# The second feed-forward walked by weight groups, with accumulators kept on chip and an order made from one stored key for each task

## Chip, cores and metric

One core of a Trainium2 chip. The metric is the device time of one execution in microseconds (us), and lower is better. The kernel before takes 879.63 us, the median of three runs (878.31 to 879.94).

## What is computed

Attention with a threshold below each row's maximum, then two feed-forward networks, one after the other, on the same 2304 tokens:

```python
scores = q @ k.T / sqrt(64)                    # 4 batches, 8 heads, 576 tokens, 64 wide
scores = where(scores >= max(scores) - tau, scores, -1e9)
x = softmax(scores) @ v                        # then heads side by side: [2304, 512]

h = x @ w_in                                   # first network, 512 -> 1024
solu = h * softmax(h)
x = layer_norm(solu) * g_ln @ w_out            # 1024 -> 512

h = x @ w2_in                                  # second network, 512 -> 2048
out = (h * tanh(softplus(h))) @ w2_out         # 2048 -> 512
```

All inputs are float32. The weights w_in, w_out, w2_in, w2_out come as 64-bit floats and are converted on chip.

## The kernel before

**Words.** A product that must keep float32 accuracy is made of three matmuls on rounded parts (high times high, low times high, high times low). A value is split by a copy on ScalarE (ACT) that rounds, and a subtraction on VectorE (DVE) or GpSimd (POOL) that leaves the low part.

**Three stages that overlap.** Attention (`s_tile`, `turn`, `pv`) writes its result to DRAM, `xd`. The first network (`moe_h`, `layer_norm`, `moe_t`, `moe_y`) reads it in tiles of 128 tokens and writes `yc`. The second network (`ff_in`, `ff_out`) is the subject of the change. Attention's early matmuls on `st` (pairs of half-height operands, 64 rows), its `pv` matmuls (half-width results, tile `V`) and all the rest are the three modes of TensorE (PE) that the planner knows.

**The second network.** Each of its two matrix products is a block product of 2x2 blocks with seven block products in place of eight. So the weights and the inputs are stored as seven combinations each: `yc` for the inputs (three units u of 768 tokens, seven tiles `y` of 768 KB for each), `w2c` for the weights. The 2048 inner columns are cut into eight groups g. `ff_in(z, g)` makes the activated combinations `gh` and `gl` of one group from seven `y` tiles and seven weight tiles `A` (256 KB each, stored as high and low words): 7 products of 6 matmuls, 128x384. `ff_out(v, q)` multiplies two groups (q is a pair of groups, 0 to 3) with 14 weight tiles `B`: 14 products of 6 matmuls. A `B` tile is stored raw (128 KB), so each load is followed by a copy on ACT (L1039) and a subtraction on DVE (L1041). The sums are added to four accumulators `acc` for a unit by DVE (L1136); the first one is a copy by ACT (L1134).

**The walk.** `VISITS` lists which unit is on chip and which pairs q it goes through:

```python
VISITS = (0, (0,1)), (1, (1,0)), (2, (0,1,2,3)), (0, (3,2)), (1, (2,3))
```

Units 0 and 1 come twice. At the end of their first visit the accumulators go to DRAM (`part`), at the start of the second they are loaded again. A set of `A` or `B` tiles is kept only from one step to the next (`AL.clear()`, `BL.clear()`). The seven `y` tiles have a ring of seven and two more, `y7x`, from the second visit on; `A` has 8 buffers, `B` 20, `acc` 5.

**The order.** No engine's order is written by hand. Each piece is a task with an engine, a duration and its needs, and `Plan.run` makes a list schedule: the engine that can start first takes the ready task with the best key, and the instructions are issued in that order. The keys come from forty turns of a forward and a backward pass, and the table `REFINE` then shifts some of them. A slot of a ring is taken to be free when the user as many places before it is done. All DMAs of the three stages are issued from one queue, SyncE's (SP), in the planned order, so a DMA that waits for its data or its buffer holds all behind it.

Of the kernel before, what the change touches and what calls it, by code (L numbers as in the profile page):

```python
# [80 lines left out]
class Plan:  # L81
# [28 lines left out]
    @staticmethod  # L110
    def lag(d, t):
        if d.eng == t.eng:
            return 0.0 if t.eng in ("PE", "-") else 0.13
        return 0.0 if d.eng == "SP" else 0.2 if d.eng == "PE" else 0.27 if t.eng == "PE" else 0.16

    def ranks(self):

        for t in self.tasks:
            t.left, t.key = len(t.out), 0.0
        ready = [t for t in self.tasks if not t.left]  # L120
        while ready:
            t = ready.pop()
            t.key += t.dur
            for d, data in t.need:
                far = (0.2 if d.eng != t.eng else 0.0) + (2.0 if d.eng == "SP" else 0.0) if data else 0.0
                d.key = max(d.key, t.key + far)
                d.left -= 1
                if not d.left:
                    ready.append(d)
# [27 lines left out]
    def moved(self, order):  # L157

        digits = "ABCDEFGHIJKLMNOPQRSTUVWXYZabcdefghijklmnopqrstuvwxyz0123456789+/"
        for z in range(0, len(REFINE), 4):  # L160
            x = 0
            for c in REFINE[z:z + 4]:
                x = 64 * x + digits.index(c)

            def draw():
                nonlocal x
                x = (x * 1103515245 + 12345) & 0x7FFFFFFF
                return x >> 8

            draw()  # L170
            middle, half, rare = draw() % len(order), 20 + draw() % 400, 1 + draw() % 5
            size = (1.0, 3.0, 10.0, 30.0)[draw() % 4]
            for t in order[max(0, middle - half):middle + half]:
                if draw() % (1 << rare) == 0:
                    t.key -= size * (draw() % 2001 - 1000) / 500.0
# [73 lines left out]
    def backward(self):  # L249

        free, port, dma, mode = {}, 0.0, 0.0, 0
        for t in self.tasks:
            t.after, t.before = [], []
# [974 lines left out]
```

## Time and profile before

| | |
|---|---|
| runs | 878.31, 879.63, 879.94 us |
| the profiled execution | span 879.3 us, from its first to its last instruction, within the range of the runs |
| TensorE (PE) matmuls | 848.3 us busy, 96% of the span |
| VectorE (DVE) | 766.1 us busy, 87% |
| ScalarE (ACT) | 609.4 us busy, 69% |
| GpSimd (POOL) | 328.9 us busy, 37% |
| DMA | 195.21 MB, 222 GB/s over the span |
| chain that ended last | PE 69%, DVE 15%, DMA 6%, ACT 4% |

The first row of the second network on PE stands at 426.7 us, the last matmul of the first network ends at 520.7 us. A PE that is busy for 96% of a span is not at its peak for that time: a matmul's row lasts longer than the distance to the next one. What counts on PE is how many matmuls there are, at what distance they follow each other, and where the row is empty.

### The profile page before, as it was taken

The numbers are of one execution on the slowest core, as the hardware profiler recorded it, in microseconds if no ns is written. First come the engines' busy times: TensorE is split into PE (matmuls) and PEld (weight loads), VectorE is DVE, ScalarE is ACT, GpSimd is POOL, SyncE is SP. The second block draws the span as 40 slices with busy tenths as digits, with TensorE's granted clock in tenths as the row PEclk, the third lists the DMA queues.
The fourth block names the chain that finished last, engine by engine and source line by source line (L and its number), as shares of the span: only waits on it lengthen the run. The fifth ranks groups of instructions, "written<-read, shape, count | busy, mean of one in ns | idle before, by whom it ended". The sixth has DMA issues, their size and how long they took to land.

```text
span 879.3 us, 16385 instructions
## 1 busy us (share of the span) xinstructions
PE 848.3 (96%) x5423; PEld 736.9 (84%) x5423; DVE 766.1 (87%) x1638; ACT 609.4 (69%) x1292; POOL 328.9 (37%) x370
## 2 busy tenths in 40 slices
PE   8899999999999999999999998999989999999998
PEld 4556666778787887978897898999989999999997
DVE  7998998879888899997778899999999997788877
ACT  5889998779878978866556867765656565455442
POOL 3677767556765574544134211112311201010100
PEclk9999999999999999999999999999999999999999
DMA  7667543354735546376996689999998768787541
GB/s 226 196 198 211 158 145 127 96 157 127 216 102 168 183 144 222 91 221 191 372 361 188 198 286 318 356 367 385 352 326 261 236 204 271 236 312 248 199 156 72
DMA packets 155573, 195.21 MB, mean 222 GB/s; under 512 B 15313, under 2 KB 112609, under 8 KB 155489
## 3 DMA queue, kind: packets, MB, share of 16 engines
q1 hardware_dynamic: 155344, 194.17, 67.9%
q8 instruction: 43, 0.70, 0.3%
q14 instruction: 42, 0.34, 0.1%
q10 hardware_dynamic: 144, 0.00, 0.0%
HBM read 142.94 MB, written 51.19 MB: 221 GB/s over the span
## 4 chain that ended last, share of the span: by engine, by line
PE 69%; DVE 15%; DMA 6%; ACT 4%; issue 3%; POOL 2%; SPq 0%; ACTq 0%; POOLq 0%; DVEq 0%
PE hoa L1012 22%; PE p_mo L846 10%; PE p_mo L916 8%; PE hob L1012 7%; PE p_ta L789 6%; PE p_ta L739 5%; PE st L702 4%; PE st L694 4%; DVE e L712 2%; DVE gl L1100 2%; DVE ws L605 2%; DVE acc L1136 1%; DVE m L708 1%; DMA B<-w2c 1%; PE p_mo L895 1%
## 5 line engine op out<-in xcount | busy, mean ns | idle before, releaser
L1012 PE MATMUL hoa<-y,A 128*128 128x384 f32 x696 | 136.3, 338 | 2.1 <-DMA A<-w2c 1.0
L1072 POOL TENSOR_TENSOR gf<-gf 128x384 f32<-128x384 f32 x24 | 33.9, 1411 | 252.7 <-DVE gf L1072 252.7
L1012 PEld LDWEIGHTS hoa<-y,A 128*128 128x128 f32 x696 | 121.9, 189 | 4.1 <-ACT gf L1062 1.8
L712 DVE SCALAR_TENSOR_TENSOR e<-st,m,e 128x576 f32<-128x576 f32 x139 | 111.2, 812 | 12.9 <-ACT e L709 7.3
L708 DVE TENSOR_REDUCE m<-st 128x1 f32<-128x576 f32 x139 | 102.3, 751 | 19.8 <-PE st L702 10.7
L709 ACT ACTIVATE e<-st,m 128x576 f32<-128x576 f32 x139 | 101.6, 744 | 20.6 <-DVE m L708 19.7
L1012 PE MATMUL hoa<-gh,B 128*128 128x384 f32 x436 | 111.5, 336 | 1.6 <-DVE acc L1136 1.4
L1100 DVE TENSOR_TENSOR gl<-gf,gh 128x384 fp32r<-128x384 f32 x168 | 93.8, 598 | 0.7 <-ACT gh L1098 0.4
L739 PE MATMUL p_ta<-ident,e 128*128 128x128 f32 x576 | 83.7, 277 | 3.5 <-DVE e L712 1.2
L916 PE MATMUL p_mo<-LH,W2H 128*128 128x256 f32 x288 | 83.9, 291 | 0.0
L739 PEld LDWEIGHTS p_ta<-ident,e 128*128 128x128 f32 x576 | 65.1, 140 | 20.9 <-ACT ey L720 3.7
L916 PE MATMUL p_mo<-LL,W2H 128*128 128x256 f32 x288 | 81.4, 283 | 0.0
L916 PE MATMUL p_mo<-LH,W2L 128*128 128x256 f32 x288 | 81.3, 282 | 0.0
L1012 PEld LDWEIGHTS hoa<-gh,B 128*128 128x128 f32 x436 | 78.4, 188 | 3.5 <-DVE acc L1136 2.8
L1098 ACT ACTIVATE gh<-gf 128x384 fp32r<-128x384 f32 x168 | 78.2, 514 | 4.4 <-DVE gf L1072 2.5
L1068 ACT ACTIVATE gf<-gf 128x384 f32<-128x384 f32 x72 | 37.5, 523 | 57.7 <-DVE gf L1065 57.6
L1012 PE MATMUL hoa<-gl,B 128*128 128x384 f32 x218 | 73.6, 337 | 3.6 <-DVE gl L1100 3.6
L711 POOL TENSOR_SCALAR m<-m,cs 128x1 f32<-128x1 f32 x144 | 51.4, 359 | 64.9 <-DVE m L708 51.0
L555 POOL TENSOR_TENSOR ws<-cf,cl 128x512 uint32<-128x512 uint32 x32 | 46.3, 1446 | 73.3 <-DMA w2c<-ws 37.5
L846 PE MATMUL p_mo<-W1H,XH 128*128 128x512 f32 x144 | 61.3, 426 | 1.8 <-DVE LL L901 1.8
L1012 PE MATMUL hob<-gh,B 128*128 128x384 f32 x236 | 60.6, 338 | 0.4 <-DVE acc L1136 0.4
L1136 DVE TENSOR_TENSOR acc<-acc,hoa 128x384 f32<-128x384 f32 x93 | 50.2, 548 | 11.4 <-PE hoa L1012 9.7
(127 smaller groups left out, 2244.1 us busy)
## 6 DMA issues: line engine op xcount, KB each, us to landing
A<-w2c SPq DMA_DIRECT2D x140, 256.0 KB
y<-yc SPq DMA_DIRECT2D x28, 768.0 KB
w2c<-ws SPq DMA_DIRECT2D x32, 448.0 KB
B<-w2c SPq DMA_DIRECT2D x112, 128.0 KB
cr<-w_in SPq DMA_DIRECT2D x32, 256.0 KB
cr<-w_out SPq DMA_DIRECT2D x32, 256.0 KB
yc<-yh SPq DMA_DIRECT2D x9, 896.0 KB
yc<-ys SPq DMA_DIRECT2D x9, 896.0 KB
```

What stands on the lines that cost most here:

```text
L708: t = add("DVE", dve(S), lambda: V.tensor_reduce(m.tile[:, 2:3], x(), AX.XY, ALU.max, negate=True), [t], [m], [st])
L709: a = add("ACT", act(S, True) + 0.1, lambda: SC.activation(et(), x(), ACTF.Exp, bias=m.tile[:, 2:3]), [t], [e] if h == 0 else (), [st, m, ...
L711: b = add("POOL", 0.26, lambda: G.tensor_scalar(m.tile[:, 1:2], m.tile[:, 2:3], -1.0, nt8, ALU.mult, ALU.add), [t], use=[m])
L712: t = add("DVE", dve(S) + 0.06, lambda: V.scalar_tensor_tensor(et(), x(), m.tile[:, 1:2], et(), ALU.is_ge, ALU.mult, accum_out=sr.tile[:, ...
L739: TE.transpose(tp.tile[:, k * 128:(k + 1) * 128], e.tile[:, o:o + 128], ident)
L789: TE.matmul(acc.tile[h * 64:h * 64 + 64, :w], v.tile[:, k, h], r, start=(k == 0), stop=(k == KT))
L846: TE.matmul(h.tile, l.tile[:, kt], r[:, kt, j * 512:(j + 1) * 512], start=(kt == 0 and x == 0), stop=(kt == KD - 1 and x == 2))
L916: TE.matmul(y.tile[:, :PN], l[:, k, cs], r.tile[:, k], start=(k == 0 and x == 0), stop=(k == KF - 1 and x == 2))
L1012: TE.matmul(x.tile[:, :TH], l, r, start=new and n == 0, stop=stop and n == len(steps) - 1, skip_group_check=True)
L1098: a = add("ACT", act(TH), lambda h=h, x=x: SC.activation(h.tile, full(x), ACTF.Copy), [first], [h], [h, x])
L1100: out[c] = h, l, add(e, cost(TH), lambda h=h, l=l, x=x, eng=eng: eng.tensor_tensor(l.tile, full(x), f(h.tile), ALU.subtract), [a, *deps], ...
L1136: d = add("DVE", dve(TH), lambda: V.tensor_tensor(to(), to(), fr(), ALU.add), deps + [CO.get((v, e, i, t))], use=[ac, x])
```

## The change

Nothing of the arithmetic changes: PE has the same matmuls in the same numbers (2016 of them in the second network). Four things change.

1. The walk. Each pair q is now visited by all units before the next pair begins, and the direction turns at the ends, so each step changes either the unit or the pair. There are nine visits instead of five. Every set of `A` and `B` tiles is loaded once (group 0 of `A` twice), the `y` tiles at each visit.
2. The buffers. Twelve accumulators stay on chip: eight in `acc`, four in the buffers `ys` and `yh` of the first network. `part` is gone. `A` has 8 buffers and 7 more (`A7x`, in the pool that opens when the first network is done), `B` 16, and `y` a single ring of seven.
3. The planner. One pass with stored keys, one for each task (`KEYS`), takes the place of forty turns and `REFINE`. A slot is free when any earlier user is done. Transfers have rates by row size, a first delay of 0.95 and a last of 1.5 us, and at most eight are under way; a change of PE's mode counts 0.24 us (before 0.1).
4. Some durations of tasks.

```diff
-    TURNS = 40
-    WAITS = 20.0, 250.0
-    ISSUE, LATENCY = 0.65, 0.92
-    LOAD, AVOID = 1.3, (3.0, 30.0, 150.0)
-    DRAIN = 0.1
+    RULE = 250.0, 3.0
+    ISSUE, FIRST, LATENCY = 0.48, 0.95, 1.5
+    LANES = 8
+    LOAD = 1.3
+    DRAIN = 0.24
...
+        for z, t in zip(range(0, len(KEYS), 3), self.tasks):
+            a, b, c = (place[k] for k in KEYS[z:z + 3])
+            t.key = (a * 4096 + b * 64 + c - 65536) / 64.0
...
+                for x in t.takes:
+                    at = max(at, min(x.buf.free, default=1.0e9))
...
-                free["SP"] = b + self.ISSUE
-                dma = max(free["SP"] + self.ISSUE, dma) + t.dur
+                dma = max(b + self.FIRST, dma) + t.dur
                 t.end = dma + self.LATENCY
+                lanes.append(t.end)
+                lanes.pop(0)
+                free["SP"] = max(b + self.ISSUE, lanes[0])
...
-    NA, NB, NL, NR, NX, NC, NF = 8, 20, 13, 14, 2, 5, 8
+    NA, NB, NL, NR, NC, NF = (8, 7), 16, 13, 14, 8, 7
...
-    b_a, b_b = (buf(p, n, [128, 2, 256], F32R, k) for p, n, k in (("fa", "A7", NA), ("fc", "B7", NB)))
-    b_y, b_yx = (buf(p, n, [128, 2, TU // PN, 2, 128], F32R, k) for p, n, k in (("fa", "y7", 7), ("fc", "y7x", NX)))
-    ring_y = [b_y] * 7
+    b_a, b_ax, b_b = (buf(p, n, [128, 2, 256], F32R, k) for p, n, k in (("fa", "A7", NA[0]), ("fc", "A7x", NA[1]), ("fc", "B7", NB)))
+    b_y = buf("fa", "y7", [128, 2, TU // PN, 2, 128], F32R, 7)
...
-    VISITS = (0, (0,1)), (1, (1,0)), (2, (0,1,2,3)), (0, (3,2)), (1, (2,3))
+    VISITS = (0, (0,)), (1, (0,)), (2, (0, 1)), (1, (1,)), (0, (1, 2)), (1, (2,)), (2, (2, 3)), (1, (3,)), (0, (3,))
...
+    for u in (0, 1):
+        for i in range(2):
+            for e in range(2):
+                ac = b_ac.new()
+                AC[u, e, i] = ac, lambda ac=ac: ac.tile
+    for e in range(2):
+        last = (b_ys, b_yh)[e].new()
+        for i in range(2):
+            AC[2, e, i] = last, lambda last=last, i=i: f(last.tile.rearrange("p c n -> p (c n)"))[:, i * TU:(i + 1) * TU]
...
-        A = AL.pop(g, None) or [load_w(b_a, 0, g, c, o_a) for c in range(7)]
-        AL.clear()
-        AL[g] = A
+        if g not in AL:
+            early = z == 0 or g % 2
+            AL[g] = [load_w(b_a if early else b_ax, 0, g, c, o_a if early else o_c) for c in range(7)]
+        A = AL[g]
...
-        Bs = BL.pop(q, None) or {(c, g): load_w(b_b, 1, g, c, o_c) for c in range(7) for g in gs}
-        BL.clear()
-        BL[q] = Bs
-        if begins:
-            for e in range(2):
-                for i in range(2):
-                    ac = AC[v, e, i] = b_ac.new()
-                    if more[0]:
-                        CO[v, e, i, 0] = CO[v, e, i, 1] = add("SP", dma(512 * TU), lambda ac=ac, e=e, i=i: D(ac.tile, part[u][e + 2 * i]),
-                                                              [PA[u, e, i], o_c], [ac])
+        if q not in BL:
+            BL[q] = {(c, g): load_w(b_b, 1, g, c, o_c) for c in range(7) for g in gs}
+        Bs = BL[q]
```

In numbers of instructions, counted in the order of both programs: `y` loads 35 and 63, `A` loads 140 and 63, `B` loads 112 and 56 and with each one copy on ACT and one subtraction on DVE, stores to `part` 8 and 0, loads from it 8 and 0. The additions to accumulators (144 on DVE, 24 copies on ACT), all else on DVE, ACT and POOL, and every matmul stand in both as often. TensorE changes its mode 125 times before and 110 times now.

**First place: PE early in attention.** L694 and L722 are the early half-height matmuls, L789 and L817 `pv`, L742 to L739 and L767, L770 transposes through `ident`. Before:

```order
L789 MATMUL p_ta_328<-ex,V 64x256 x8
L789 MATMUL p_ta_328<-eu,V 64x256 x2
L742 MATMUL p_ta_356<-ident,e 128x128
L694 MATMUL s_360<-Kst,Qhh 128x256
L694 MATMUL s_360<-Kst,Qhh 128x320
L739 MATMUL p_ta_368<-ident,e 128x128 x4
L739 MATMUL p_ta_379<-ident,e 128x128 x4
L694 MATMUL st<-Kst,Qhh 128x320
L694 MATMUL st<-Kst,Qhh 128x256 x2
L694 MATMUL st<-Kst,Qhh 128x320
L742 MATMUL p_ta_406<-ident,e 128x128
```

And of the change, at the same place of the program:

```order
L817 MATMUL p_ta_324<-ex,V 64x256 x8
L817 MATMUL p_ta_324<-eu,V 64x256 x2
L767 MATMUL p_ta_356<-ident,e 128x128 x4
L767 MATMUL p_ta_364<-ident,e 128x128 x4
L722 MATMUL s_375<-Kst,Qhh 128x256
L722 MATMUL s_375<-Kst,Qhh 128x320
L722 MATMUL st<-Kst,Qhh 128x320
L722 MATMUL st<-Kst,Qhh 128x256 x2
L722 MATMUL st<-Kst,Qhh 128x320
L770 MATMUL p_ta_394<-ident,e 128x128
```

The transposes no longer stand between two groups of half-height matmuls: five changes of mode have become three.

**Second place: PE where the first network ends and the first `ff_out` begins.** L916 and L944 are the last matmuls of the first network, L1012 and L1039 the second network's. Before:

```order
L916 MATMUL p_mo_6786<-LL,W2H 128x256
L1012 MATMUL hoa_6020<-y_5783,A_6624 128x384 x6
L1012 MATMUL hoa_6895<-y_5678,A_6681 128x384 x6
L1012 MATMUL hoa_6020<-y_5802,A_6672 128x384 x6
L1012 MATMUL hoa_6736<-y_5794,A_6644 128x384 x6
L1012 MATMUL hoa_6941<-y_5688,A_6699 128x384 x6
L1012 MATMUL hoa_6955<-y_5738,A_6792 128x384 x6
L1012 MATMUL hoa_6988<-gh,B_6893 128x384 x2
L1012 MATMUL hoa_6988<-gl,B_6893 128x384
```

And of the change:

```order
L944 MATMUL p_mo_6797<-LL,W2H 128x256
L1039 MATMUL hoa_6242<-y_5963,A_6581 128x384 x6
L1039 MATMUL hoa_6001<-y_5974,A_6623 128x384 x6
L1039 MATMUL hoa_6878<-y_6731,A_6028 128x384 x6
L1039 MATMUL hoa_6750<-y_6253,A_6013 128x384 x6
L1039 MATMUL hoa_6928<-y_6086,A7x 128x384 x6
L1039 MATMUL hob_6945<-y_6240,A7x 128x384 x6
L1039 MATMUL hoa_6750<-y_6757,A_6560 128x384 x6
L1039 MATMUL hob_6977<-gh,B_6861 128x384 x2
L1039 MATMUL hob_6977<-gl,B_6861 128x384
```

Seven products of `ff_in` instead of six now stand ahead of the first one with `B`, and the fifth and sixth of them read `A7x`, whose pool, like that of `B`, opens only when the first network is done.

**Third place: PE in the middle of the second network, where one `y` tile follows another in the same buffer.** `y_9467` of unit 2 takes the buffer that `y_9062` of unit 1 leaves. Of the change:

```order
L1039 MATMUL hoa_9233<-y_9062,A_8685 128x384 x6
L1039 MATMUL hoa_9458<-gh,B_8990 128x384 x2
L1039 MATMUL hoa_9458<-gl,B_8990 128x384
L1039 MATMUL hoa_9458<-gh,B_8995 128x384 x2
L1039 MATMUL hoa_9458<-gl,B_8995 128x384
L1039 MATMUL hoa_9233<-y_9110,A_8725 128x384 x6
L1039 MATMUL hoa_9480<-y_9271,A_9383 128x384 x6
L1039 MATMUL hoa_9233<-y_9137,A_8762 128x384 x6
L1039 MATMUL hoa_9257<-y_9123,A_8750 128x384 x6
L1039 MATMUL hoa_9515<-y_9467,A7x 128x384 x6
```

Between the last matmul on the old tile and the first on the new one stand 30 matmuls. Eight of the 56 reloads of `y` have 30 to 36 matmuls between, the others more. Before, the ring of nine left two tiles to run ahead.

## Rows read from the trace of the kernel before

**Rows 1.** Stretches of core 0: busy us by engine, granted clock, DMA share, GB/s

```profile
0.00:175.00 175.00, 164.93 (x1088) 107.76 (x1090) 155.53 (x337) 147.23 (x301) 111.85 (x160) 1.00 0.55 170
175.00:417.00 242.00, 236.89 (x1728) 199.12 (x1726) 212.35 (x453) 192.82 (x390) 138.61 (x156) 1.00 0.54 165
417.00:528.00 111.00, 108.28 (x703) 98.00 (x701) 90.99 (x202) 71.39 (x136) 30.18 (x22) 1.00 0.84 280
528.00:550.00 22.00, 19.46 (x101) 18.96 (x101) 19.85 (x44) 16.70 (x42) 2.50 (x2) 0.92 0.93 319
550.00:700.00 150.00, 144.91 (x818) 141.02 (x817) 145.20 (x314) 94.48 (x220) 30.42 (x21) 1.00 0.96 326
700.00:880.00 180.00, 173.84 (x996) 172.03 (x994) 142.17 (x293) 86.74 (x207) 15.32 (x12) 1.00 0.64 213
```

**Rows 2.** Waits of PE from 525 to 880 us: total, times, longest

```profile
PE hoa L1012 <- DVE gl L1100: 3.6, 3, 2.5
PE hoa L1012 <- ACT gf L1062: 1.4, 2, 0.9
PE hoa L1012 <- DVE acc L1136: 1.4, 2, 0.9
PE hoa L1012 <- DMA A<-w2c: 1.0, 1, 1.0
PE hob L1012 <- ACT gf L1062: 0.9, 1, 0.9
```

**Rows 3.** The chain that ended last, in order of time, 520 to 535 us

```profile
522.29 4.78 DMA B<-w2c
...
527.10 0.77 ACT B L1039 x2
...
530.47 0.48 DVE gl L1100
```

**Rows 4.** Groups of instructions on DVE, 550 to 700 us: busy, mean ns

```profile
L1100 DVE TENSOR_TENSOR gl<-gf,gh 128x384 fp32r<-128x384 f32 x70 | 41.1, 630 | 0.1
L1041 DVE TENSOR_TENSOR B<-B 128x256 fp32r<-128x256 f32 x44 | 19.6, 464 | 0.0
...
L605 DVE TENSOR_TENSOR ws<-ws 128x128 f32<-128x128 f32 x45 | 12.6, 282 | 0.1
```

**Rows 5.** DMA issues over the whole span, with KB each

```profile
A<-w2c SPq DMA_DIRECT2D x140, 256.0 KB
y<-yc SPq DMA_DIRECT2D x28, 768.0 KB
...
B<-w2c SPq DMA_DIRECT2D x112, 128.0 KB
...
part<-acc SPq DMA_DIRECT2D x8, 384.0 KB
```

**Rows 6.** A lone load: SP's timeline 791 to 794 us

```profile
792.26 0.32 SPq L1028 DMA_DIRECT2D y<-yc  x1
```

**Rows 7.** DMA by 40 slices of 0.125 us, 792 to 797 us

```profile
DMA  2210000005699910919697999929241040999095
```

**Rows 8.** The chain, 740 to 757 us

```profile
743.23 6.17 DMA y<-yc
...
750.48 5.92 DMA A<-w2c
```

**Rows 9.** Timeline of weight loads at a change of mode, near 11 us

```profile
10.92 0.30 PEld L694 LDWEIGHTS st<-Kst,Qhh 64*128 64x128 f32 x4 [0.17 <-issue]
```

**Rows 10.** Waits of weight loads, 0 to 525 us

```profile
PEld st L694 <- issue: 10.7, 30, 2.5
```

**Rows 11.** The chain, 690 to 712 us

```profile
697.79 7.28 PE hoa L1012 x42
```

More of the change, by code (lines that the diff above doesn't have):

```diff
@@ L111, in lag @@
     def lag(d, t):
[L112 to L129, printed above, removed]
+        if d == t:
+            return 0.0 if t in ("PE", "-") else 0.13
+        return 0.0 if d == "SP" else 0.2 if d == "PE" else 0.27 if t == "PE" else 0.16
     def place(self, choose, put, first):
@@ L214, in put @@
                 bank[x.bank] = None
+            for x in t.takes:
+                x.buf.free.remove(min(x.buf.free))
             if t.port:
@@ L234, in put @@
                     stale.add("PE")
+            for x in t.drops:
+                x.held -= 1
+                x.latest = max(x.latest, t.end + max(self.lag(t.eng, e) for e in x.buf.eng))
+                if not x.held:
+                    x.buf.free.append(x.latest)
+                    stale.update(x.buf.eng)
             for k in t.opens:
@@ L247, in forward, with run @@
         return done if self.place(choose, put, first) else None
[L249 to L251 removed]
+    def run(self):
+        self.shared, self.banks, self.groups, self.rings, self.slots = [], [], [], [], []
         for t in self.tasks:
[L253 to L301 removed]
@@ L303, in run @@
-    def run(self):
-        self.shared, self.banks, self.groups = [], [], []
-        for t in self.tasks:
-            t.bank, t.back, t.uses, t.out, t.leads, t.opens = None, None, [], [], [], []
+            t.bank, t.back, t.uses, t.out, t.opens, t.takes, t.drops = None, None, [], [], [], [], []
         for t in self.tasks:
@@ L318, in run @@
                     continue
-                if x.k >= b.bufs:
-                    t.need += [(u, True) for u in b.slots[x.k - b.bufs].users]
+                t.takes.append(x)
+                self.slots.append(x)
+                for u in x.users:
+                    u.drops.append(x)
                 if x.k:
                     t.need.append((b.slots[x.k - 1].taker, False))
+                if b not in self.rings:
+                    self.rings.append(b)
+                    b.eng = set()
+                b.eng.add(t.eng)
         for k in self.banks:
@@ L588, in words7 @@
             out.append((a, b))
-        return [add("SP", dma(128 * 7 * n * 4), lambda w=w, y=y: D(dst(w), f(y.tile)), [o[w] for o in out], use=[y]) for w, y in ((0, hi), (1, x))]
+        return [add("SP", dma(128 * 7 * n * 4, n * 4), lambda w=w, y=y: D(dst(w), f(y.tile)), [o[w] for o in out], use=[y]) for w, y in ((0, hi), (1, x))]
     WLO = V, "DVE", dve
@@ L1158, in ff_out @@
                     r0 = (e + 2 * i) * 128
-                    to = (lambda e=e, i=i: part[u][e + 2 * i]) if more[1] else (lambda r0=r0: out[r0:r0 + 128, u * TU:(u + 1) * TU])
-                    PA[u, e, i] = add("SP", dma(512 * TU), lambda e=e, i=i, to=to: D(to(), AC[v, e, i].tile),
-                                      [CO[v, e, i, t] for t in range(2)], use=[AC[v, e, i]])
+                    add("SP", dma(512 * TU, 4 * TU), lambda e=e, i=i, r0=r0: D(out[r0:r0 + 128, u * TU:(u + 1) * TU], AC[u, e, i][1]()),
+                        [CO[u, e, i, t] for t in range(2)], use=[AC[u, e, i][0]])
     MINUS = [{'D': ('DVE', dve(TH)), 'P': ('POOL', gps(TH))}[k] for k in 'DPDD']
@@ L1168 @@
         for q in qs:
-            for g in (2 * q + 1, 2 * q) if q == qs[0] and z else (2 * q, 2 * q + 1):
+            for g in (1, 0) if z == 1 else (2 * q, 2 * q + 1):
                 ff_in(z, g)
             ff_out(z, q)
+            if z == 0:
+                AL.pop(0)
     plan.run()
```

303 lines of the change are left out of this document (165 added, 138 removed).

## Prediction

> **What bounds the kernel now.** I read the stretches first. PE is busy almost throughout: in six stretches [rows 1] it is empty for 10.1, 5.1, 2.7, 2.5, 5.1 and 6.2 us (each stretch less its busy time), 31.7 us in 880, of which the last few are the final stores. The matmuls of the second network follow each other at 7.28 / 42 = 0.173 us [rows 11], and the change takes none away. So PE's work is the floor, and only its waits, its mode changes and a low clock can be won: some 30 us at most, plus whatever hides inside rows that count as busy.
>
> Who is waited for differs by stretch. From 550 to 700 us DVE is busy for 145.2 of 150 us and the DMA engines for 0.96 of the time, at 326 GB/s [rows 1]: both are full where PE loses its 5.1 us. The list of PE's waits in the second network [rows 2] names DVE (gl, acc) and ACT (gf), and only once a DMA, 1.0 us for an A tile. The chain shows the start of that stage: the first B tiles, 4.78 us of DMA, their copy on ACT, then gl [rows 3]. PE's longest wait there, 2.5 us [rows 2], comes right before the only stretch with a low clock: 0.92 granted over 22 us [rows 1]. With levels of 2.4 and 1.2 GHz that is 22 x 0.08 / 0.5 = 3.5 us at the lower one, so about 1.8 us lost.
>
> **The change part by part**, against the profiled execution's own 879.3 us (the median of the runs is 879.63, so nothing is to be added).
>
> *Traffic.* A loads fall by 77 of 256 KB, B loads by 56 of 128 KB, 16 transfers of 384 KB to and from part go, and 28 loads of y at 768 KB are added [rows 5]: -20.2 - 7.3 - 6.3 + 22.0 = -11.8 MB of 195. That is 36 us of a full DMA at 326 GB/s, but only a single 1.0 us wait of PE is put down to an A load [rows 2]: I count **-1.0** for it, and the room goes to the y loads below.
>
> *DVE and ACT.* 56 subtractions of B go, and as many copies on ACT. In the full stretch 44 of the 112 stand, 0.464 us each [rows 4]; half of them are 10 us of 145. It is not all gain: the conversions of the second network's weights (L605 and others, [rows 4]) now run on until the last pair is needed, so some move into the stretch where B left. What PE waited for DVE and gf outside the first 2.5 us is 1.1 + 1.4 + 1.4 + 0.9 = 4.8 us [rows 2]. Bounds 0 and -4.8; DVE should fall from 97% to about 91%, which thins the waits without ending them: I take **-3.0**. On ACT, 69% busy overall, the copies cost nothing now, being covered by ACT's slack.
>
> *First ff_out.* Before, 36 matmuls (6.2 us) separate the end of the first network from the first product with B; now 42 (7.3 us), and the B chain has 1.0 us more. But the two A7x products stand 24 and 30 matmuls behind that end, 4.2 and 5.2 us. Their loads open at the same event as B's and take the next places on SP. A B load took 4.78 us there [rows 3], so the first A7x is likely to be 1 to 2 us late. Before, 2.5 us of wait and 1.8 us of clock were lost; I keep 2.0: **-2.3** (bounds -4.3 and +1, the latter if the wait is as long again and the clock falls as before).
>
> *The y ring of seven.* This is where the change adds a wait. Eight reloads have 30 to 36 matmuls, 5.2 to 6.2 us, between the last use of the old tile and the first of the new. What a load takes is in two rows: alone on the queue, issued at 792.26 [rows 6], its bytes move until slice 33 of 40, 796.1 us [rows 7]: 3.9 us. Behind others it was 6.17 us until the waiting step was released [rows 8]. So a reload costs 0 or about 1.0 us, 0 to 8 in all; behind it the whole product queue on PE waits, then gf and gl. Reloads with more matmuls between are covered by the ff_out between them, 84 matmuls or 14.6 us, against 7 x 0.79 MB / 326 GB/s = 16.9 us of transfer for a whole unit, spread over a longer time since tiles come free one by one. Most loads there meet others on the queue, but less than before: I take **+3.0**.
>
> [...]
>
> *Mode changes.* 15 fewer. A weight load right after a change stood idle for 0.17 us [rows 9]; over the 30 waits of this kind the mean is 10.7 / 30 = 0.36 us [rows 10]. So 2.6 to 5.4 us; I take the lower, since the larger mean also holds other waits: **-2.6**.
>
> *The new order of the first 528 us.* Attention and the first network do the same work in another order. PE is empty there for 10.1 + 5.1 + 2.7 = 17.9 us [rows 1]. DVE is at 89% in the first 175 us, so the softmax chain is the limit and no order removes it all. The planner's transfers are nearer to the lone load above (a first delay of 0.95 us; in [rows 7] the bytes start in slice 9, at 793.1, 0.87 us after the issue), which should help, but the order was found on a model all the same. Bounds: half the idle time won, -9, or 5 lost. I take a quarter, **-4.5**.
>
> *At no cost:* the copy and addition counts are equal, and the accumulators in ys and yh only need the first network to be done with them, which it is before the first ff_out of unit 2.
>
> Sum: -1.0 - 3.0 - 2.3 + 3.0 - 2.6 - 4.5 = -10.4, so 879.3 - 10.4 = **868.9 us**.
>
> **The rivals.**
>
> *The y reloads are the new bound (slower).* The nine buffers were two tiles of slack, now there is none, and each of the nine visits reloads all seven tiles. For it: a load behind another 768 KB takes 2.4 us more at 326 GB/s, and an A tile of a third the size took 5.92 us behind y loads [rows 8]. Against it: rows 2 name no y load as a wait now, and 11.8 MB are gone. If each of the eight reloads is late by 1.0 us and half a load more, 2.2 us, and two visits in addition lose 2 us at wider gaps, the term is 21.6 instead of 3: 887.5 us. It decides from a term of 13.4 us on, 1.7 us for each of the eight.
>
> The Trainium skill speaks on the same side: "Double-buffer for performance" ("Trainium Kernel Development and Optimization", Best Practices). As a mechanism of this kernel that is the case just worked out; no row of before can show it, since the ring of nine ran ahead.
>
> *DVE stays the limit.* The conversions fill the room that B leaves, and the early order gives only 2 us: -1.0 - 2.3 + 3.0 - 2.6 - 2.0 = -4.9, so 874.4 us. For it: DVE at 97% [rows 1] with many kinds of work; against it: 56 x 0.464 = 26 us less in all.
>
> *Everything works.* All of DVE's waits go, no y load is late, and half of the early idle time is won: -1.0 - 4.8 - 4.3 - 2.6 - 9.0 = -21.7, so 857.6 us. For it: the y loads start as early as the lone one, and the DMA is emptier. Against it: it needs three terms at their ends.
>
> *Nothing to measure.* The early order loses what the second network wins: a term of +5 there instead of -4.5 gives 878.4 us.
>
> **How the numbers follow.** The forecast's own case, 863 to 873 us, gets 0.44. Everything works, under 863: 0.18. DVE the limit, 873 to 877.9: 0.13. Within 0.2% (1.8 us, about what a measurement of this kernel can tell from no change): 0.08. Slower, by the y reloads or by an early order that is worse: 0.17. So faster 0.75, same 0.08, slower 0.17. The range leaves out a tenth at each end: under 857, where three terms stand at their best ends, and over 883, where the y term is near 17 us. It is 857 to 883; that of the likeliest case is 863 to 873.
>
> **What would show it.** In the profile of the changed kernel: about 26 us less DVE busy and less on ACT by 56 copies, and DVE in the middle of the second network near 91%, with fewer waits for gl and acc. Waits of PE for y loads, new, a few of about 1 us, 3 us in total; much more of them is the first rival. A wait of 1 to 2 us for A7x at the end of the first network, and no stretch there with a lower clock. 110 mode changes, and an idle time of PE in the first 528 us near 13 us. The forecast is wrong if the early idle time has grown, since no row of before tells how good the new order is, or if waits for y reach 1.7 us each.

## The result and the profile after

The changed kernel takes 886.38 us (median of six runs, 884.39 to 887.89) where the kernel before takes 878.97: a ratio of 1.0087, 95% interval 1.0065 to 1.0109. It is slower by some 7.4 us; the forecast was 868.9, and 886 lies outside its range. One of the six runs before, 1035.49 us, is a slow one that the ratio leaves out; without it the median before is 878.31. The profiled execution spans 884.4 us, before 879.3.

The stretches up to 700 us, as in [rows 1]:

```profile
0.00:175.00 175.00, 162.84 (x1083) 109.89 (x1083) 151.70 (x329) 142.72 (x289) 113.61 (x156) 1.00 0.55 171
175.00:417.00 242.00, 237.90 (x1715) 199.36 (x1716) 214.88 (x456) 198.43 (x400) 137.71 (x157) 1.00 0.53 161
417.00:528.00 111.00, 103.92 (x684) 92.89 (x683) 79.96 (x175) 63.41 (x126) 29.42 (x20) 0.98 0.80 270
528.00:550.00 22.00, 18.44 (x102) 18.12 (x101) 17.83 (x32) 15.71 (x37) 3.65 (x3) 0.92 0.96 327
550.00:700.00 150.00, 147.69 (x836) 144.02 (x835) 139.07 (x294) 89.61 (x195) 26.35 (x20) 1.00 0.82 277
```

PE is empty for 12.2, 4.1, 7.1, 3.6 and 2.3 us there; before it was 10.1, 5.1, 2.7, 2.5 and 5.1. In the first 528 us that makes 23.4 us in place of 17.9. The second network at 550 to 700 us got better, as forecast, with an emptier DMA and a DVE at 139 of 150 us. The stretch from 417 to 528 us got worse by 4.4 us, and the clock is low in two stretches (0.98 and 0.92) in place of one: in the trace it stands at the lower of its two levels for 3.4 us from 520.6 us on, behind a wait of 1.9 us, and again for 3.4 us from 537.7 us on, behind a wait of 3.6 us.

PE's waits from 525 us on, as in [rows 2]:

```profile
PE hoa L1039 <- ACT gf L1096: 4.1, 2, 3.6
PE hoa L1039 <- DMA y<-yc: 1.0, 2, 0.9
...
PE hob L1039 <- DMA y<-yc: 0.4, 1, 0.4
```

So PE's wait for `gl`, which hung on `B` before [rows 2, 3], is gone, waits for y loads come to 1.4 us, and a new one of 3.6 us stands first. What it is made of is in the chain around it (start, duration, what):

```profile
529.72 1.06 PE hoa L1039 x6
...
533.02 1.27 DVE gf L1106
534.29 1.55 DVE gl L1134
...
535.86 0.50 ACT gf L1096
...
536.40 1.90 PE hoa L1039 x8
```

PE has no more to do until ACT has copied a first product of the next `ff_in` group (L1096, `copy`), and that copy waits for `gl` of the group before. What `gl` sets free is a `gf` buffer. ACT's own waits from 410 to 560 us name the same pair; before there is no such row in that stretch:

```profile
ACT gf L1096 <- DVE gl L1134: 4.0, 3, 2.2
```

And before that, PE's waits from 417 us on have five of 0.7 us or more in the first network (lines 874 and 923). They are for the layer norm's result (`so`, L904), for the low part of the network's input (`XL`, L863) and for two copies of PE's results out of their banks (L957, L881):

```profile
PE p_mo L923 <- POOL so L904: 2.5, 2, 1.3
PE p_mo L923 <- ACT ys L957: 1.0, 1, 1.0
PE p_mo L874 <- POOL XL L863: 0.7, 1, 0.7
PE p_mo L923 <- ACT so L881: 0.7, 1, 0.7
```

**Where the time went.** Both profiles hold 5423 matmuls. If each record counts with the usual distance of its form to the next one (0.173 us for `ff_in` and `ff_out`, 0.228 for L874 and 0.120 for L944, and so on), the records give how far PE has come, and the time lost is the time passed less the work done; PE's waits are in it, and what a low clock costs. From one profile each, with the runs told of below:

```
time lost (us) when PE has done ... us of its work
                                 400    475    500    550    650    800
before                          41.3   45.0   50.2   50.8   58.7   60.7
changed                         40.2   50.8   56.4   57.0   62.3   66.7
e1_gf8                          39.9   51.0   54.3   54.9   59.3   63.9
e3_head                         42.1   48.1   50.6   51.7   57.1   62.6
e4_head_gf8                     40.2   45.9   50.0   51.0   54.3   59.9
e8_fillers                      40.0   45.1   47.6   49.2   53.7   58.9
s2_new_walk_searched            44.3   47.2   52.6   53.8   56.1   57.3
x1_join_406                     41.5   44.7   49.9   51.3   54.3   55.5
```

400 us of work are the attention and some of the first network (440 us of time), 475 about its end, 475 to 500 the junction, where the first `ff_out` begins. Up to 400 the changed kernel is 1.1 us ahead; from 400 to 475 it loses 10.6 us where before lost 3.7; in the junction 5.6 against 5.2; from 550 on 9.7 against 9.9. Each low spell of 3.4 us is an estimated 1.7 us of this (half of it): one in the 10.6, one in the 5.6, and one in the 5.2 of before. A start can differ by 2 us between executions (e3 and e4 walk the same order up to 400), so differences between columns tell more than a column.

### The profile page after: what moved, and what is told of

Read it like the earlier page. It is cut to its first block, busy times and chain, and to the rows that moved or that the text cites. A ratio compares the mean times of both kernels' runs of the same rounds, so it can differ in the third digit from the quotient of the medians.

```text
span 884.4 us, 16090 instructions
## 1 busy us (share of the span) xinstructions
PE 849.1 (96%) x5423; PEld 739.0 (84%) x5423; DVE 753.4 (85%) x1582; ACT 596.3 (67%) x1234; POOL 330.7 (37%) x370
## 2 busy tenths in 40 slices
DMA packets 138146, 183.39 MB, mean 207 GB/s; under 512 B 13376, under 2 KB 103504, under 8 KB 138064
## 4 chain that ended last, share of the span: by engine, by line
PE 65%; DVE 16%; ACT 8%; DMA 5%; issue 3%; POOL 2%; SPq 1%; DVEq 0%; POOLq 0%; ACTq 0%
PE hoa L1039 22%; PE p_mo L944 9%; PE hob L1039 8%; PE p_mo L874 8%; PE p_ta L817 5%; PE p_ta L767 4%; PE st L730 4%; PE st L722 3%; DVE e L740 2%; DVE gl L1134 2%; ACT e L737 2%; DMA y<-yc 1%; DVE m L736 1%; PE p_mo L923 1%; DMA Qhh<-qq 1%
## 5 line engine op out<-in xcount | busy, mean ns | idle before, releaser
L1039 PE MATMUL hoa<-gh,B 128*128 128x384 f32 x488 | 124.5, 335 | 1.0 <-DVE acc L1161 0.6
L1106 POOL TENSOR_TENSOR gf<-gf 128x384 f32<-128x384 f32 x24 | 29.4, 1226 | 229.7 <-DVE gf L1106 229.7
L1132 ACT ACTIVATE gh<-gf 128x384 fp32r<-128x384 f32 x168 | 82.6, 519 | 28.1 <-DVE gf L1106 14.0
L1039 PEld LDWEIGHTS hoa<-gh,B 128*128 128x128 f32 x488 | 87.7, 188 | 2.6 <-DVE acc L1161 1.5
L767 PE MATMUL p_ta<-ident,e 128*128 128x128 f32 x576 | 82.8, 276 | 6.4 <-ACT ex L748 2.8
L1039 PE MATMUL hoa<-y,A 128*128 128x384 f32 x402 | 81.0, 343 | 6.4 <-ACT gf L1096 6.1
L944 PE MATMUL p_mo<-LH,W2H 128*128 128x256 f32 x288 | 84.5, 293 | 0.1
L767 PEld LDWEIGHTS p_ta<-ident,e 128*128 128x128 f32 x576 | 65.4, 140 | 22.7 <-ACT ex L748 5.7
L1039 PE MATMUL hoa<-gl,B 128*128 128x384 f32 x244 | 81.7, 335 | 0.0
L944 PE MATMUL p_mo<-LH,W2L 128*128 128x256 f32 x288 | 81.5, 283 | 0.0
L944 PE MATMUL p_mo<-LL,W2H 128*128 128x256 f32 x288 | 81.4, 283 | 0.0
L739 POOL TENSOR_SCALAR m<-m,cs 128x1 f32<-128x1 f32 x144 | 52.6, 368 | 74.8 <-DVE m L736 68.5
L1039 PEld LDWEIGHTS hoa<-y,A 128*128 128x128 f32 x402 | 70.8, 191 | 9.0 <-ACT gf L1096 7.3
L1039 PE MATMUL hoa<-y,A7x 128*128 128x384 f32 x342 | 69.1, 339 | 1.0 <-DMA y<-yc 0.9
L1039 PEld LDWEIGHTS hoa<-y,A7x 128*128 128x128 f32 x342 | 60.4, 189 | 2.4 <-DVE gf L1099 2.1
L874 PE MATMUL p_mo<-W1H,XH 128*128 128x512 f32 x144 | 61.0, 424 | 0.2 <-DVE ln L896 0.2
```

The costliest lines, as they stand in the source:

```text
L739: b = add("POOL", 0.26, lambda: G.tensor_scalar(m.tile[:, 1:2], m.tile[:, 2:3], -1.0, nt8, ALU.mult, ALU.add), [t], use=[m])
L767: TE.transpose(tp.tile[:, k * 128:(k + 1) * 128], e.tile[:, o:o + 128], ident)
L874: TE.matmul(h.tile, l.tile[:, kt], r[:, kt, j * 512:(j + 1) * 512], start=(kt == 0 and x == 0), stop=(kt == KD - 1 and x == 2))
L944: TE.matmul(y.tile[:, :PN], l[:, k, cs], r.tile[:, k], start=(k == 0 and x == 0), stop=(k == KF - 1 and x == 2))
L1039: TE.matmul(x.tile[:, :TH], l, r, start=new and n == 0, stop=stop and n == len(steps) - 1, skip_group_check=True)
L1132: a = add("ACT", act(TH), lambda h=h, x=x: SC.activation(h.tile, full(x), ACTF.Copy), [first], [h], [h, x])
```

## The experiments

The theories: (A) the ring of `gf`. The line of the buffer counts, `NF`, went from 8 to 7, and a group takes 7. (B) The new order of the first part. (C) The stretch is simply full. Rival from the prediction: the reloads of y. A ratio is to the kernel before, run beside the run in question, with its 95% interval. The runs were made at different times, so a difference of two medians is softer than its digits: going by the widths of the intervals, it takes some 2 us to tell two kernels apart.

Several runs fix the order. For these the keys are replaced by places, and each engine takes its steps in exactly that order (no cost of the planner decides any more, only the PSUM bank):

```diff
-            t.key = (a * 4096 + b * 64 + c - 65536) / 64.0
+            t.key = a * 4096 + b * 64 + c
+        self.turn = {e: sorted((t for t in self.tasks if t.eng == e), key=lambda t: -t.key) for e in self.ORDER}
...
-            now, best = free.get(e, 0.0), None
+            now, best, c = free.get(e, 0.0), None, [t for t in c if t is self.turn[e][-1]]
```

**e1: an eighth buffer, nothing moved.**

```diff
-            self.tile = b.pool().tile(b.shape, b.dtype, tag=b.tag, name=b.tag, bufs=b.bufs)
+            self.tile = b.pool().tile(b.shape, b.dtype, tag=b.tag, name=b.tag, bufs=8 if b.tag == "gf" else b.bufs)
```

> The changed kernel, every instruction in the same place, with eight gf buffers in place of seven. Theory A (the ring of gf): in the changed kernel TensorE waits 2.1 us at 517.8 and 3.7 us at 532.5 for ScalarE's first copy of a group, which itself waits until VectorE has formed the last low half of the group before and so freed the seventh gf buffer; both waits should fall below 1 us, and one of the two low-clock spells (3.4 us at half clock each) should go with them: 3 to 6 us faster, so 880.5 to 883.5. Theory B (the order of the first 490 us is the cause): no more than 1.5 us faster. Theory C (ScalarE and VectorE are simply full in that stretch): the wait moves on to the high and low halves, within 1 us of 886.4.

883.79 us, 2.6 less by the medians (ratio to before 1.0064, 1.0042 to 1.0085) and some 2.0 by the ratios, whose intervals overlap. The second low clock is gone, and in place of the long wait in the junction stand two of 1.2 us. Its stretch from 528 us, and PE's waits for the copy from 525 us on and from 417 to 560 us:

```profile
528.00:550.00 22.00, 19.54 (x114) 18.58 (x113) 19.98 (x37) 17.51 (x41) 3.81 (x3) 1.00 0.96 319
...
PE hoa L1039 <- ACT gf L1096: 3.1, 3, 1.2
...
PE hoa L1039 <- ACT gf L1096: 4.4, 3, 1.9
```

Theory A holds for this part, a little under the size expected; the wait of 1.9 us that ends at 520 us stays, and so does the low clock behind it. From 475 to 500 the loss is 3.3 us in place of 5.6. Most of that is the clock: the waits there fall by 1.1 us, from 3.56 to 2.45, and the low spell was an estimated 1.7. The other runs agree: the mean granted clock of the changed kernel's six is 0.9947, of these six 0.9980.

**e3 and e4: the first part in the order of before**, with seven and with eight buffers. Edit: only the table of places. The steps of the second network keep the changed kernel's order among themselves and are fitted in between.

> The changed kernel with seven gf buffers, but the attention, the first network and the weight conversions that belong to them (3134 of 4822 steps) in the order that the kernel before has for them on each engine; the rest keeps the order of the changed kernel among itself and is fitted in between. Theory B (the new order of the first 490 us makes transposes of the first network wait for the layer norm, 5.6 us in five waits between 436 and 487 us against 1.6 us in two before): those waits fall back to about 1.6 us, and the time falls by 3 to 5 us, to 881.5 to 883.5. Theory A: the first network is not dearer, the gf waits stay, within 1.5 us of 886.4. The fitting in of the rest may cost some us by itself between 500 and 560 us; then the stretch up to the last matmul of the first network (529.4 in the changed kernel, 520.5 before) tells more than the whole time.

> The kernel with the first part in the order of before, and eight gf buffers as well. If theories A and B are both true and add up, 6 to 10 us faster than the changed kernel (876 to 880), so about as fast as the kernel before. If only one is, as fast as the better of the two single edits.

e3: 881.44 us, 4.9 less than the changed kernel (ratio to before 1.0034, 1.0012 to 1.0055); e4: 879.39 (1.0021, 1.0004 to 1.0037), 7.0 less. The two about add up (2.6 and 4.9 against 7.0 us; by the ratios 2.0 and 4.7 against 5.8). The waits for `so` on POOL are gone from 417 to 560 us of e3, and shorter ones for `LL`, the low part of the layer norm's result, stand beside the wait for the copy:

```profile
PE hoa L1039 <- ACT gf L1096: 2.1, 1, 2.1
PE p_mo L923 <- DVE LL L929: 1.5, 2, 0.8
...
PE p_mo L874 <- DVE LL L929: 0.9, 1, 0.9
```

Theory B is the larger half, theory C falls: the same work of the same engines loses 5.7 us from 400 to 475 in e4, 10.6 in the changed kernel, of which an estimated 1.7 is the low clock from 520.6 us on. Before lost 3.7 there, so the order is not back in full. The mean granted clock of the runs is 0.9978 in e3 and 0.9983 in e4: against 0.9947 that is an estimated 3.2 us of 884 in e4, nearly half of its gain. Since each of the two edits alone takes most of the low clock away, their prices can't be parted cleanly into waits and clock.

**e5 and e10: half the bytes of y**, first on the changed kernel, later on e8 (below).

```diff
-  f(y.tile.rearrange("p w z k n -> p (w z k n)")), yc[u][c].rearrange(...)
+  f(y.tile.rearrange("p w z k n -> p (w z k n)"))[:, :2 * TH], yc[u][c].rearrange(...)[:, :2 * TH]
...
-  lambda: [y.tile[:, m, :, k] for _, m in words for k in range(2)]
+  lambda: [y.tile[:, 0, :, k] for _, m in words for k in range(2)]
```

> The changed kernel with half of the bytes of each y load (63 loads of 393 KB in place of 786 KB: only the high words are loaded, and the matmuls that want the low words read the high ones), same instructions in the same order. If the reloads of y into one ring of seven are what makes the change slow (the first rival of the prediction), 8 us or more faster. If the waits for y in the profile (1.4 us in all) are all that they cost, 0.5 to 2.5 us faster. If the heavier DMA traffic around 530 to 700 us also holds back other loads, 2.5 to 5 us.

> The kernel with the first part in the order of before, eight gf buffers and the five moved steps (878.34), with half of the bytes of each y load (the matmuls that want the low words read the high ones). On the changed kernel the same edit gave 3.2 us. If the price of y stands by itself, again 2.5 to 3.5 us, to 875 to 876; if it was a price of the late junction, under 1.5 us.

The low words of y are left out. 883.17 us, 3.2 less (1.0064, 1.0039 to 1.0088), and 875.87, 2.5 less than e8 (0.9970, 0.9951 to 0.9990); by the ratios 2.0 and 3.1. The first rival falls: halving the bytes gives back 2 to 3 us, not 8. On the changed kernel the list of waits puts 1.4 us down to y, and where the rest sits is not shown. In e8 the waits for y from 525 us on come to 2.8 us, and in e10 none is left, so there they account for the gain. What the other half of the bytes costs, and what a ring of nine would give, no run shows.

**e6 and e9: VectorE's saved work put back**, on e4. e6 has 168 small subtractions, e9 has 94 of them; the edit shown is e6's.

```diff
+    def again(v, d):
+        if v in (1, 3, 5, 7):
+            d.fn = lambda go=d.fn: (go(), *(V.tensor_tensor(top, top, top, ALU.subtract) for _ in range(3)))
...
-            CO[u, e, i, t] = d
+            CO[u, e, i, t] = d; again(v, d)
```

> The kernel with the first part in the order of before and eight gf buffers (879.39), with VectorE's saved work put back: in four of the nine visits, behind each of the 14 accumulations of the group, three subtractions of 128x88 on a tile that nobody else uses (about as long as one 128x256 subtraction of 0.46 us), so 56 times 0.46 us, 26 us of VectorE's time, with no load and no wait of their own. It computes nothing more. If the relief of VectorE is worth what the prediction gave it (3.0 us, between 0 and 4.8), 2.5 to 4.8 us slower, 882 to 884. Rival: VectorE has slack enough in that stretch, at most 1 us slower.

> The earlier run that put VectorE's work back overshot: its subtractions of 128x88 took 276 ns each in place of some 155, 46.4 us in all where 26 were meant. Here 94 of them in place of 168, so 26 us. If the loss is in proportion to VectorE's time once it is the limit of the stretch, 26/46 of 31 us, 15 to 19 us slower than 879.39; if a part of the 26 us still fits into VectorE's idle time, as the prediction had it (3.0 us, bound 4.8), 3 to 8 us slower.

e6: 910.73 us, 31 more (1.0371, 1.0340 to 1.0402). The work put back was larger than meant, 46.4 us in place of 26:

```profile
L1139 DVE TENSOR_TENSOR top<-top 128x88 f32<-128x88 f32 x168 | 46.4, 276 | 3.8
```

e9: 892.85 us, 13.5 more (1.0158, 1.0120 to 1.0195; by the ratios 12.0), between the two ranges expected, with 27.7 us put back:

```profile
L1140 DVE TENSOR_TENSOR top<-top 128x88 f32<-128x88 f32 x94 | 27.7, 295 | 1.3
```

PE's new waits in e9 are many and short (528 to 890 us):

```profile
PE hoa L1039 <- ACT gf L1096: 4.9, 4, 2.0
PE hoa L1039 <- DVE acc L1166: 2.4, 5, 0.8
PE hoa L1039 <- DVE gf L1099: 2.2, 3, 1.4
PE hob L1039 <- DVE gf L1099: 2.1, 2, 1.3
```

So nearly half of the work put back turns up in the time, about four times what the prediction gave for its removal. It is no measure of what the 56 subtractions cost before, where the planner placed them; here each stands right behind an accumulation.

**e7 and e8: moved by hand**, on e4. In e7 two roundings of y on ACT (L614) go behind the next copies; in e8 three products on PE go in front of transposes as well. Only the table changes.

> The kernel with the first part in the order of before and eight gf buffers (879.39), with two of ScalarE's roundings of y (1.05 and 0.83 us, line 614) moved behind the first two copies of the next ff_in group. What is left of TensorE's waits at the junction is one of 2.0 us at 527.6, on a copy that ScalarE runs only after those two. If the order on ScalarE is its whole cause, that wait falls under 0.5 us and the time by 1.5 to 2 us, to 877.4 to 877.9. If something else also ends there (VectorE, a PSUM bank), by less than 0.7 us.

> The kernel before this one in the list, and on TensorE three pieces moved by a few places so that they run in front of transposes that wait for the layer norm (waits of 0.98, 1.27 and 0.88 us at 447, 475 and 483): two ff_in products of 1.04 us and one sixth of a first-network product of 0.7 us. If those waits are only a matter of the order, 2 to 3 us faster than it: 874.5 to 876, and so faster than the kernel before (877.97). If the pieces leave a wait of the same size where they stood, no change.

e7: 880.50 us (1.0025, 1.0007 to 1.0044), e8: 878.34 (1.0005, 0.9988 to 1.0022). The wait on the copy falls from 2.0 to 1.1 us in e7, but its time does not fall. e8 is 2.2 us faster than e7, as expected of its three pieces, and 1.1 us faster than e4, with intervals that overlap in both cases; 874.5 to 876 is missed, since e7 gave nothing. It equals the kernel before.

**w0 and w2: both walks under one planner**, the old one without its table. The durations of tasks that it reckons with stay those of each kernel, so walk and durations change together. w0 is the kernel before without `self.moved(best[1])`; w2 is the changed kernel with that `Plan` and

```diff
-    NA, NB, NL, NR, NC, NF = (8, 7), 16, 13, 14, 8, 7
+    NA, NB, NL, NR, NC, NF = (8, 7), 16, 13, 14, 8, 8
```

> The kernel before without its table of shifts (the order is what its own planner finds in 40 turns): old walk, old planner. It is the reference for the next run. Expected some us slower than the kernel before, 880 to 895; no theory hangs on this alone.

> The changed kernel's walk and its buffers, but eight gf buffers, planned by the planner of the kernel before without a table: new walk, old planner. Theory D (the walk itself is worth what the prediction's terms for it sum to: traffic 1.0, VectorE 3.0, junction 2.3, y -3.0): 2 to 5 us faster than the run with the old walk and the same planner. Theory E (the walk is even or worse by itself: y takes back what VectorE gains): between 1 us faster and 5 us slower than that run.

w0: 898.64 us (1.0242, 1.0197 to 1.0286), w2: 894.80 (1.0182, 1.0148 to 1.0216). The new walk is 3.8 us faster, with intervals that overlap, so this is not clear of noise; w0 is slower than the 880 to 895 expected. And the table of before is worth 20 us: an order can weigh more than either walk.

**e11: are a few places the cause?** e1 with three `ff_in` products moved on PE.

> The changed kernel with eight gf buffers (883.79) and its own order, but for three ff_in products of 1.04 us each that are moved by a few places on TensorE, in front of transposes of the first network that wait for the layer norm (waits of 1.45, 1.33 and 0.86 us at 452, 482 and 484). If those waits are what the new order of the first part costs, 2.5 to 3.5 us faster: 880.3 to 881.3. If the three products leave waits of the same size where they stood, within 1 us of 883.8.

882.71 us (1.0079, 1.0049 to 1.0109), 1.1 less than e1 by the medians and no better by the ratios. So fixing the order by places costs nothing that these runs can see. The profile is of the slowest of its six runs, 888.05 us. In it, from 417 to 560 us the waits only change places: `so` gives 2.3 of its 2.5 us back, and `ln`, the small factors of the layer norm, and `LL`, the low part of its result, come to 2.9:

```profile
PE p_mo L874 <- DVE ln L896: 1.9, 1, 1.9
...
PE p_mo L944 <- DVE LL L929: 1.0, 1, 1.0
...
PE p_mo L923 <- POOL so L904: 0.2, 1, 0.2
```

So three places on PE alone don't cure it. That the layer norm as a whole comes late in this order fits these waits, but is not shown.

**s0, s2, s3: orders searched anew**, for either walk: 1.2 million trials for the new one, 0.28 million for the old one, which started from the order of the kernel before.

> New walk, its buffers with eight gf buffers, and an order searched anew: starting from the order of the run with the new walk and the old planner, random shifts of the steps' keys are kept where the old planner's own forward pass ends no later (some 1.2 million trials); the kernel then walks each engine's steps in exactly that order. If the prediction's sum for the walk holds and only the orders were at fault (the walk alone measured 3.8 us faster than the old one under one planner), an order as good as that of the kernel before gives 872 to 876, faster than it (878.2). If the walk is even by itself, 877 to 880. If searched orders don't carry over to the chip, 880 or more.

> The same as the run before it in the list, from another random seed: how far two orders that the planner holds for equally good lie apart on the chip. Expected within 3 us of it.

> The old walk with the same kind of search, starting from the order of the kernel before (some 0.28 million trials, no further gain in the last third): the control. If the search itself is worth something on the chip, faster than the kernel before by as much as that; expected 876 to 879. What the new walk is worth is then read against this run.

s2: 878.34 us (1.0014, 0.9996 to 1.0033), s3: 878.85 (1.0003, 0.9979 to 1.0027), s0: 876.93 (1.0001, 0.9980 to 1.0022). Against the 894.80 of w2 the search gave 16 us, but both walks end where the kernel before is. By the table above s2 loses only 3.5 us from 550 to 800, where before lost 9.9 and s0, by the same reckoning, 7.4: with both orders searched the new walk's second network is 3.9 us better, though the searches were not equal. From 400 to 550 it loses 9.5 us, s0 7.6, and the start takes the rest.

**x1, x2, x3: the first part of e8 with the rest of s2**, joined at three places.

> New walk, eight gf buffers; the first 2600 of 4822 steps (up to about 406 us, all of the attention) in the order of the run with five moved steps, the rest in the searched order. If the searched order's second network (3.5 us lost from 604 to 857 us, against 9.9 us in the kernel before over the same work) is what the walk gives and its first part is merely no better than the other's, 874 to 877; if the join costs waits of its own, 878 or more.

> The same with the join at step 3100 (about 505 us, most of the first network in the order of the run with five moved steps). That order had lost 47.6 us when TensorE had done 500 us of its work, the searched one loses 4.7 us from there on: if both keep what they had, 60.7 less 52.3, some 8 us faster than the kernel before: 870 to 873. If the join at the busiest place costs what it gains, 876 to 880.

> The same with the join at step 3200 (about 524 us, the whole first network in the order of the run with five moved steps). Expected as the run with the join at 505 us: 870 to 873 if both parts keep what they had, 876 to 880 if the join costs it.

x1: 875.35 us (0.9969, 0.9950 to 0.9987); x2: 878.74 (0.9997, 0.9980 to 1.0015); x3: 881.68 (1.0034, 1.0019 to 1.0048). x1 is faster than both kernels, 2.6 us than that before; it keeps s2's good second network (4.2 us lost from 550 to 800). The joins at 505 and 524 us, of which 870 to 873 was hoped, lose that again. In x1 the longest waits after 525 us are for y, and for B as in [rows 3]:

```profile
PE hoa L1039 <- DMA y<-yc: 2.0, 2, 1.4
PE hoa L1039 <- ACT B L1072: 1.9, 1, 1.9
PE hoa L1039 <- DVE B L1074: 1.4, 1, 1.4
```

## Why the prediction was wrong

**The step that failed: the new order of the first 528 us, -4.5 (bounds -9 and +5)**, and with it the mode changes, -2.6. Together they had 7.1 us won there; the changed kernel has lost 5.8 us more than before when PE has done 475 us of its work. Up to 400 us it is 1.1 us ahead, less than the 2 us by which a start can differ. The mode changes did fall from 125 to 110, but e3 and e4, which have the 125 of before, have lost 42.1 and 40.2 us there against its 40.2: no gain by them shows. The loss is in the first network. Putting the order of before back gives 4.9 us. The prediction read the first 528 us as idle time of which a quarter could be won, though most of it lay in the first 175 us; the stretch from 417 to 528 had only 2.7 us to win [rows 1] and much to lose, and the order was given as a table that no row of before could price. A quarter of the idle time was a hope, not a reading. What exactly makes PE wait in the first network in the new order is not settled: e11 shows that moving three products doesn't cure it.

**The first ff_out, -2.3 (bounds -4.3 and +1): right event, wrong buffer.** No wait of PE names B's chain or A7x, in the changed kernel or in e1, and yet the wait is longer than before, 3.6 us against 2.5, since `NF` went from 8 to 7 and the prediction passed over that number in the diff. With the eighth buffer the junction (475 to 500) loses 3.3 us where before lost 5.2: -1.9, close to the term. The ring of seven costs 2.6 us in the time, most of it as low clock. The clock was told wrongly too: two low spells in place of none.

**The y ring of seven, +3.0: about the right size.** Half the bytes gave 2 to 3 us, which prices the bytes and not the ring by itself. The changed kernel has three waits of 1.4 us together, not the rival's 1.7 us each.

**DVE, -3.0.** B's rows on DVE fell from 45.9 to 23.5 us, by 22.4 where 26 was worked out, and DVE's busy time only from 766.1 to 753.4; where the other 10 us went is not shown:

```profile
PE 849.1 (96%) x5423; PEld 739.0 (84%) x5423; DVE 753.4 (85%) x1582; ACT 596.3 (67%) x1234; POOL 330.7 (37%) x370
```

From 550 us of work on, where this term and y's both act, the changed kernel loses 9.7 us, before 9.9: +3.0 and -3.0 cancel, as the sum had it. The term was no upper limit, though: with better orders the same walk loses 3.5 and 4.2 us there. By subtraction, and only so, with y at its measured 2.5 to 3.2 us, what is saved is worth some 3 us in the order given; against the 7.4 us that the searched old walk loses there, some 6 to 7 in the searched ones.

**Traffic, -1.0.** The loads fell as counted, 183.39 MB, and no wait for A is left:

```profile
y<-yc SPq DMA_DIRECT2D x63, 768.0 KB
...
A<-w2c SPq DMA_DIRECT2D x35, 256.0 KB
```

**Sum.** Ring and order together give back 7.0 of the 7.4 us (e4; by the ratios 5.8 of 7.6, and e4 is still 1.0021 of before); what the walk itself gives and takes comes to about nothing in that order, where the prediction had -3.3. It had counted on no low spell at all; an estimated 3.2 us of the 7.0 are the clock. The rival that ends on the slower side named y; its place was wrong. "The forecast is wrong if the early idle time has grown" was the right sentence: it grew from 17.9 to 23.4 us, and the order's price of 4.9 us is at the bound of +5. The rival "Nothing to measure" had this price and still came to 878.4, since it kept the gains of the second network, the junction and the mode changes.

## What to carry to other kernels

Read every number in a line of buffer counts against what one step takes at once: a ring with exactly as many slots as one group needs makes consecutive groups wait for each other, and the wait shows up as the copy that opens the next group, released by the last reader of the one before. A change that replaces the table behind a schedule is two changes: here one walk's orders, with and without the planner's table of shifts, lay 20 us apart, so ask of each which stretch has idle time to win and which has cover to lose. A saving in one stretch is kept only if the order there is made for it: the same walk with the same buffers lost 9.7 (e8) or 3.5 us (s2) in the second network, depending on nothing but the order. And look at the clock behind each new wait of TensorE: here it was an estimated 3.2 of the 7.0 us that the repair gave back.

## Unexpected of the hardware

Subtractions of 128x88 on DVE took 276 and 295 ns on the mean and 249 and 245 in the median (e6, e9), where the 128x256 one, with almost three times the elements, takes 437 on the mean, and 467 from 550 to 700 us (L1074 in the changed kernel). And DVE's extra time came back at half its size in the kernel's time at 27.7 us, at two thirds at 46.4 us, although DVE had stood idle for 11.5 of the 150 us from 550 on in e4, to which it was added. After the wait of 3.6 us in the changed kernel the granted clock was 0.92 over 22 us, which is 3.5 us at the lower of its two levels, as before behind its wait of 2.5 us; in e1 the longest wait there is 1.2 us and the granted clock 1.00, so the eighth buffer took away both. Runs of one kernel differ in this too: over the 296 runs that give the ratios here, one that shows 1 us less of full clock than the mean of its kernel is an estimated 0.8 us longer.
